# One tile per turn of TensorE's summing loop, its address in a register, instead of four tiles with constant addresses

## The chip, the core and the metric

The kernel runs on one core of one Trainium2 chip. The metric is the device time of the program in microseconds (us), taken from the slowest core, of which there is one. Kernels are compared only within the same rounds. A ratio is the mean time of one kernel's runs over the mean of the other's runs of the same rounds, so it is not quite the ratio of the medians that are quoted. The profile's span is about 1.8 us shorter than the time.

In the profile lines PE is TensorE, PEld its weight loads, DVE VectorE, ACT ScalarE, POOL GpSimd and SP SyncE. A q behind a name marks records of that engine's sequencer, the part that handles waits, register and branch instructions and the issue of DMAs; these do not count as busy time. L236 is line 236 of the kernel. `arena` is the on-chip buffer with the four slots.

## The reference

Every channel of a 384 x 384 x 384 picture in bfloat16 is scaled by a gate, which is a sigmoid of the channel's mean times one weight:

```python
def reference(x, w1d):                 # x: (1, 384, 384, 384), w1d: (1,)
    g = jnp.einsum("bhwc->bc", x) / (H * W)
    s = _sigmoid(g * w1d[0])           # k = 1, so the padding and the loop fall away
    return x * s[:, None, None, :]
```

The gate depends on all of x, so a plain program reads x twice. This one does not.

## The kernel before

It guesses. It takes the mean of the first 12 of 1152 rows (a row is 128 x 384 elements), computes the gate `s_early` from it, and gates and stores all of x with that, while TensorE sums all of x. At the end it computes the true gate `s_true`, rounded to bfloat16, and compares the two. Only where they differ does a second pass run; with these inputs they agree. So x is read once and written once: 226.5 MB in all.

The rows after the first 12 are 19 tiles of 60 rows. A tile is loaded by SyncE's DMA queue into one of four slots, summed by TensorE (45 matmuls of 128 x 512 against a matrix of ones, accumulated in three PSUM banks), gated in place by VectorE in two parts, and stored through ScalarE's queue. GpSimd tells TensorE with a semaphore `ready` that a tile has landed. VectorE may gate a part only when TensorE has summed it, and a slot is loaded again only when its store has landed. The last tile is gated into a free slot, so that it does not wait for TensorE.

The part of TensorE that the change touches:

```python
def add_rows(e, group, column, n, at_bank, start, stop):
    n_wide = n * C // WIDE                      # WIDE = 512
    for i in range(n_wide):
        out = mm(e, acc[group][(at_bank + i) % 3][:, :], ones[:],
                 arena[:, column + i * WIDE : column + (i + 1) * WIDE], ...)
    return out

def one(e, s):                                  # one tile; slot(s) is a constant
    e.wait_ge(ready, 1).then_inc(ready, -1)
    for r, n in parts:                          # 28 and 32 rows
        add_rows(e, 1, (slot(s) + r) * C, n, 0, False, False).then_inc(
            plan.sems["tensor"], 1)

with e.Fori(0, rounds) as k:                    # 5 rounds
    for s in range(some):                       # 3 tiles
        one(e, s)
    with e.If(k < rounds - 1):                  # a fourth in all but the last round
        for s in range(some, SLOTS):
            one(e, s)
```

At the end, ScalarE reads the flag of the comparison and then waits for the stores:

```python
second_pass("scalar", e)        # wait for the comparison, load the flag, branch
for token in plan.final:        # then one wait per store semaphore, two at a time
    e.wait_ge(*token)
```

## Time and profile before

| | before |
|---|---|
| time, median of 3 runs | 531.79 us (531.5 to 532.03) |
| span in the profile | 530.1 us |
| TensorE / VectorE busy | 43% / 46% |
| DMA, 13 to 509 us | share 1.00, 428 to 436 GB/s |
| last load landed, last sum begun | 509.0 us |
| flag computed | 526.8 us |
| last store landed | 529.6 us |

From the page of the kernel before: the span, the busy time of each engine, the busy tenths of the 16 DMA engines in 40 slices, and the DMA queues (queue, kind: packets, MB, share of 16 engines).

```profile
span 530.1 us, 1079 instructions
...
PE 227.4 (43%) x857; PEld 0.2 (0%) x2; DVE 241.5 (46%) x57; ACT 2.7 (1%) x4; POOL 0.3 (0%) x6
...
DMA  8999999999999999999999999999999999999996
...
q10 hardware_dynamic: 3314, 121.90, 53.2%
q1 hardware_dynamic: 2880, 104.60, 45.9%
q8 instruction: 1, 0.02, 0.0%
q14 instruction: 2, 0.02, 0.0%
```

The nines say that DMA is the limit from one end to the other. The q8 line, one packet of 0.02 MB, is an instruction fetch.

The table of stretches of the kernel before (from:to in us, its length, busy us with the number of instructions for PE, PEld, DVE, ACT and POOL, TensorE's granted clock as a share of full speed, DMA share, GB/s):

```profile
13.00:60.00 47.00, 26.84 (x103) 0.00 (x0) 24.25 (x11) 0.61 (x1) 0.00 (x0) 0.78 1.01 433
...
300.00:400.00 100.00, 47.62 (x177) 0.00 (x0) 45.62 (x8) 0.00 (x0) 0.00 (x0) 0.73 1.00 433
...
480.00:509.00 29.00, 0.00 (x0) 0.00 (x0) 10.83 (x3) 0.00 (x0) 0.00 (x0) 0.56 1.01 436
509.00:522.00 13.00, 12.92 (x48) 0.00 (x0) 6.52 (x1) 0.00 (x0) 0.00 (x0) 0.81 0.97 419
522.00:530.00 8.00, 0.03 (x1) 0.00 (x0) 3.79 (x9) 0.61 (x1) 0.00 (x0) 0.64 0.50 214
```

A DMA share of 1.00 beside a TensorE that is busy less than half of the time means that TensorE has slack in the middle. The end is another matter. The timeline of the kernel before from 505 us on (start, length, what; in brackets the idle time before it and what ended it), followed by ScalarE's ten waits for the stores:

```profile
508.96 6.56 DVE L199 TENSOR_TENSOR arena<-arena,s_early 128x12288 bf16<-128x12288 bf16 x1 [16.54 <-DMA arena<-in_x_dram]
509.08 12.30 PE L236 MATMUL acc<-arena,ones 128*128 128x512 bf16 x45 [31.13 <-PEq L275]
515.55 0.34 ACTq L109 DMA_DIRECT2D out_dram<-arena  x1
521.22 0.81 PE L236 MATMUL acc<-zeros,ones 128*128 128x512 bf16 x3
...
526.63 0.15 DVE L434 CAST redo<-wrong 128x1 int32<-128x1 f32 x1
```

```profile
L489 ACTq EVENT_SEMAPHORE  x10: 38/38/38, 527.8 to 529.6; - x10
```

Two chains run side by side from the moment that the last tile lands at 509.0. One is VectorE's gate (6.56 us) and the last store, issued at 515.55 and landed at 529.6. The other is TensorE's sum of the last tile, the closing matmuls, VectorE's and ScalarE's comparison, and the flag, done at 526.8; ScalarE then loads the flag and reaches its waits at 527.8. Nine of them are passed by 528.76; the last is passed at 529.65, when the store has landed. The page's own chain of waits names the flag's chain, since ScalarE's waits do not count as work; the time of the last wait shows which of the two was later.

### The profile page before, as it was taken

The numbers are of one execution on the slowest core, as the hardware profiler recorded it, in microseconds if no ns is written. First come the engines' busy times: TensorE is split into PE (matmuls) and PEld (weight loads), VectorE is DVE, ScalarE is ACT, GpSimd is POOL, SyncE is SP. The second block draws the span as 40 slices with busy tenths as digits, with TensorE's granted clock in tenths as the row PEclk, the third lists the DMA queues.
The fourth block names the chain that finished last, engine by engine and source line by source line (L and its number), as shares of the span: only waits on it lengthen the run. The fifth ranks groups of instructions, "written<-read, shape, count | busy, mean of one in ns | idle before, by whom it ended". The sixth has DMA issues, their size and how long they took to land. (4 is left out here: it accounts for less than half of the span.)

```text
span 530.1 us, 1079 instructions
## 1 busy us (share of the span) xinstructions
PE 227.4 (43%) x857; PEld 0.2 (0%) x2; DVE 241.5 (46%) x57; ACT 2.7 (1%) x4; POOL 0.3 (0%) x6
## 2 busy tenths in 40 slices
PE   2284971052434436262717080908080808070053
PEld 0000000000000000000000000000000000000000
DVE  0353997008080907172625353445344443538142
ACT  1000000000000000000000000000000000000000
POOL 0000000000000000000000000000000000000000
PEclk9786987568686958585858585859686868777567
DMA  8999999999999999999999999999999999999996
GB/s 361 445 445 404 408 445 438 421 431 435 445 428 428 431 435 445 431 424 435 435 445 431 424 428 442 445 428 428 428 442 445 424 431 424 445 420 458 418 421 299
DMA packets 6197, 226.53 MB, mean 427 GB/s; under 512 B 690, under 2 KB 690, under 8 KB 690
## 3 DMA queue, kind: packets, MB, share of 16 engines
q10 hardware_dynamic: 3314, 121.90, 53.2%
q1 hardware_dynamic: 2880, 104.60, 45.9%
q8 instruction: 1, 0.02, 0.0%
q14 instruction: 2, 0.02, 0.0%
HBM read 113.25 MB, written 113.25 MB: 427 GB/s over the span
## 5 line engine op out<-in xcount | busy, mean ns | idle before, releaser
L199 DVE TENSOR_TENSOR arena<-arena,s_early 128x10752 bf16<-128x10752 bf16 (+2 forms) x39 | 234.8, 6063 | 264.2 <-PE acc L236 245.3
L236 PE MATMUL acc<-arena,ones 128*128 128x512 bf16 x849 | 224.9, 429 | 285.0 <-PEq L275 283.6
L309 DVE TENSOR_TENSOR total<-total,acc 128x128 f32<-128x128 f32 (+2 forms) x11 | 4.5, 409 | 6.9 <-PE acc L236 6.5
L307 DVE COPY total<-acc 128x384 f32<-128x384 f32 x1 | 0.6, 558 | 11.4 <-PE acc L236 11.4
L234 PE MATMUL acc<-arena,ones 128*128 128x512 bf16 x1 | 0.6, 606 | 7.6 <-DMA arena<-in_x_dram 7.6
L412 ACT ACTIVATE s_true<-total,w_scaled 128x384 bf16<-128x384 f32 x1 | 0.6, 614 | 507.6 <-DVE total L309 507.6
L236 PE MATMUL acc<-zeros,ones 128*128 128x512 bf16 x6 | 2.3, 505 | 0.0
L338 ACT ACT_TABLE_LOAD x1 | 1.3, 1283 | 2.2 <-issue 2.2
L344 PE MATMUL w_all<-w_one,ones 1*128 1x1 bf16 x1 | 0.2, 158 | 2.0 <-DMA w_one<-in_w1d_dram 2.0
L420 DVE TENSOR_TENSOR total<-s_true,s_early 128x384 f32<-128x384 uint16 x1 | 0.6, 559 | 0.7 <-ACT s_true L412 0.7
L353 DVE TENSOR_SCALAR w_scaled<-w_all 128x1 f32<-128x1 f32 x2 | 0.2, 154 | 1.3 <-PE w_all L344 1.3
L375 ACT ACTIVATE s_early<-total,w_scaled 128x384 bf16<-128x384 f32 x1 | 0.6, 614 | 12.9 <-DVE total L309 12.9
L428 DVE TENSOR_REDUCE wrong<-total 128x1 f32<-128x384 f32 x1 | 0.6, 553 | 0.0
L362 DVE MEMSET ones<- 128x128 bf16 x1 | 0.2, 165 | 0.8 <-PEq L512 0.8
L338 ACT ACTIVATE warm<-warm 128x1 f32<-128x1 f32 x1 | 0.2, 203 | 0.0
L434 DVE CAST redo<-wrong 128x1 int32<-128x1 f32 x1 | 0.2, 153 | 0.0
L234 PEld LDWEIGHTS acc<-arena,ones 128*128 128x128 bf16 x1 | 0.1, 105 | 7.7 <-DMA arena<-in_x_dram 7.7
L344 PEld LDWEIGHTS w_all<-w_one,ones 1*128 1x128 bf16 x1 | 0.1, 101 | 2.0 <-issue 2.0
L512 POOL MEMSET const-bfloat16-1.0<- 128x1 bf16 x1 | 0.1, 101 | 0.0
L512 POOL MEMSET const-uint8-127<- 128x1 uint8 x1 | 0.1, 101 | 0.0
L361 POOL MEMSET zeros<- 128x2 bf16 x1 | 0.1, 99 | 0.0
L360 POOL MEMSET warm<- 128x1 f32 x1 | 0.1, 98 | 0.3 <-POOLq L512 0.3
(2 smaller groups left out, 0.2 us busy)
## 6 DMA issues: line engine op xcount, KB each, us to landing
out_dram<-arena ACTq DMA_DIRECT2D x18, 5760.0 KB, 53.5
arena<-in_x_dram SPq DMA_DIRECT2D x16, 5760.0 KB, 35.4
arena<-in_x_dram SPq DMA_DIRECT2D x2, 3072.0 KB, 37.3
arena<-in_x_dram ACTq DMA_DIRECT2D x1, 5760.0 KB, 45.1
out_dram<-arena ACTq DMA_DIRECT2D x1, 3072.0 KB, 14.1
arena<-in_x_dram ACTq DMA_DIRECT2D x1, 2688.0 KB, 18.7
arena<-in_x_dram SPq DMA_DIRECT2D x1, 2688.0 KB, 28.5
out_dram<-arena ACTq DMA_DIRECT2D x1, 2688.0 KB, 29.9
```

The lines of the kernel that those rows point to most:

```text
L199: return lambda e: e.tensor_tensor(to_v, v, s_b, ALU.mult)
L234: loaded.append(e.matmul(bank, weights, moving, start=start, stop=stop))
L236: return e.add_instruction(mybir.InstMatmult(name=nc.get_next_instruction_name(), engine=mybir.EngineType.PE, ins=[e.lower_ap(moving), e.l ...
L307: emit = lambda e, part=part, of=of: e.tensor_copy(part, of)
L309: emit = lambda e, part=part, of=of: e.tensor_tensor(part, part, of, ALU.add)
L338: lambda e: e.activation(warm[:, 1:2], warm[:, 0:1], ACT_F.Sigmoid),
L344: lambda e: e.matmul(w_all[:, 0:1], ones[0:1, :], w_one[0:1, 0:1], start=True, stop=True),
L353: lambda e, i=i, n=n: e.tensor_scalar_mul(w_scaled[:, i : i + 1], w_all[:, 0:1], 1.0 / float(P * n)),
L375: lambda e: e.activation(s_early[:], total[:], ACT_F.Sigmoid, scale=w_scaled[:, 0:1]),
L412: lambda e: e.activation(s_true[:], total[:], ACT_F.Sigmoid, scale=w_scaled[:, 1:2]),
L420: lambda e: e.tensor_tensor(total[:], s_true[:].bitcast(U16), s_early[:].bitcast(U16), ALU.not_equal),
L428: lambda e: e.reduce_max(wrong[:], total[:], axis=mybir.AxisListType.X),
```

## The change

Its intent is a short program: one tile in the loop body instead of four, with the tile's place in a register, so that TensorE's program is 115 instructions. The alignment of its start to a fetch block is dropped as no longer needed.

```diff
-    plan = Planner(nc, "a", 50)
+    plan = Planner(nc, "a", 60)
@@ add_rows
-                arena[:, column + i * WIDE : column + (i + 1) * WIDE],
+                arena[:, bass.ds(column + i * WIDE, WIDE)],
@@ sum_others
-            rounds = -(-n_tiles // SLOTS)
-            some = n_tiles - (rounds - 1) * SLOTS
-            with e.Fori(0, rounds) as k:
-                for s in range(some):
-                    one(e, s)
-                if some < SLOTS:
-                    with e.If(k < rounds - 1):
-                        for s in range(some, SLOTS):
-                            one(e, s)
+            with e.Fori(0, n_tiles) as k:
+                e.wait_ge(ready, 1).then_inc(ready, -1)
+                column = e.snap((k & (SLOTS - 1)) * (TILE * C))
+                for r, n in parts:
+                    add_rows(e, 1, column + r * C, n, 0, False, False).then_inc(
+                        plan.sems["tensor"], 1
+                    )
@@ tensor
-            e.addr_align(256, max_nops=0)
             plan.emit("tensor", e)
```

In the built program each of the 45 matmuls is preceded by one fused register instruction (add the offset, multiply by 2 to bytes, add the base) and takes its address from a register. All other engines keep their instructions and their order.

## The prediction

> **What bounds it now.** The DMA. In the table of stretches its share is 1.00 from 13 to 509 us; TensorE is busy 43% of the 530.1 us span. A tile's 45 matmuls take 10.5 to 13 us (timeline), tiles come 27 us apart. A store takes 53.5 us (median) from issue to landing while one is issued every 27 us, so about one whole store stands in the queue ahead of it: an estimated 25 us of slack before a later TensorE starves the DMA.
>
> Only the end depends on TensorE. The last tile lands at 509.0; its matmuls run from 509.08 to 521.2, three closing ones to 522.0, VectorE's and ScalarE's chain to 526.78; then ScalarE reads the flag (0.47 us), a fused register instruction (0.18), and from 527.75 to 529.65 its ten waits for the stores. Ten waits alone take about 0.8 us, so TensorE's chain has about 1.2 us of slack behind the last store.
>
> **What changes.** Five rounds of four (or three) tiles with constant addresses become 19 rounds of one. Bytes, matmuls, loads, gates, stores and the other engines' order stay. Added on TensorE's sequencer (the built program shows it): before each of the 45 matmuls a fused register instruction of three operations, and a matmul whose address is in a register; per tile one AND and one branch (0.08 to 0.21 us in the trace). The shorter program saves nothing visible: three instruction fetches in all, no stall at the branches.
>
> **Cost of issue.** Before, from the wait for a tile to the instruction after its 45 matmuls took 3.6 to 4.3 us: 80 to 95 ns per matmul, far ahead of the array (427 ns a matmul for the first dozen at clock 0.5, then 216). A fused instruction of three operations took 177 ns on ScalarE, 186 on SyncE; TensorE's sequencer leaves about 60 ns between instructions (two moves of 35 ns start 94 apart). Estimate: 180 + 60 + 90 = 330 ns a pair, more if a register address slows the matmul or this sequencer is slower (its semaphore events take 51 ns against 38): 370 taken, 300 to 450 possible. That exceeds 216, so TensorE becomes bound by its sequencer: 45 x 0.37 = about 16.7 us a tile. The wait blocks the sequencer, so nothing is done ahead.
>
> **On the critical path.** In the middle, +4 to 6 us per tile vanishes in idle time and the store queue's slack. At the end the last tile grows by about 4.8 us; minus 1.2 of slack, the end moves by 3.6 us. The Trainium skill ("TensorE: Matmul & The Clock Gate", "The two states you'll see") says that an idle array halves its clock; this trace agrees (0.5 at each tile's start). Gaps might keep it there; then 427 ns a matmul: 19.2 us, +6 us.
>
> **Predicted:** 535.4 us, 8 times in 10 between 532.0 and 539.5. Faster by over 2%: 0.01; within 2%: 0.93; slower by over 2%: 0.06.
>
> **What would show it.** Sequencer records of 177 to 260 ns between matmuls; tiles of 15 to 19 us in the timeline; DMA share still 1.00; in the chain that ended last, the last tile 15 to 19 us instead of 13. Wrong if tiles still take 11 to 12 us (then within 1 us of before), if a register matmul costs over 500 ns (over 2% slower), or if the loop straddles a fetch block and each branch waits for the busy DMA.

## The result and the profile after

The kernel after took 533.85 us (532.0 to 533.98, 4 runs) beside 531.91 us before (531.5 to 532.04, 4 runs): ratio 1.003, interval 1.0007 to 1.0052. That is within 2%, as forecast, and inside the range, but about half of the 3.6 us that the prediction derived. The profile shows that even this half did not come from where the prediction put it.

The same lines of the page of the kernel after:

```profile
span 532.1 us, 1984 instructions
...
PE 222.5 (42%) x852; PEld 0.2 (0%) x2; DVE 241.5 (45%) x57; ACT 2.7 (1%) x4; POOL 0.3 (0%) x6
...
DMA  9999999999999999999999999999999999999995
...
q10 hardware_dynamic: 3314, 121.90, 53.0%
q1 hardware_dynamic: 2880, 104.60, 45.8%
q14 instruction: 2, 0.02, 0.0%
```

The q8 fetch is gone. The table of stretches after, still with the DMA at 1.00 in the middle:

```profile
13.00:60.00 47.00, 24.85 (x95) 0.00 (x0) 21.13 (x5) 0.51 (x1) 0.00 (x0) 0.71 1.01 432
...
300.00:400.00 100.00, 44.94 (x176) 0.00 (x0) 45.07 (x8) 0.00 (x0) 0.00 (x0) 0.76 1.00 431
...
480.00:509.00 29.00, 0.53 (x2) 0.00 (x0) 12.25 (x3) 0.00 (x0) 0.00 (x0) 0.51 1.00 431
509.00:522.00 13.00, 11.34 (x47) 0.00 (x0) 7.11 (x5) 0.00 (x0) 0.00 (x0) 0.91 0.96 413
522.00:532.00 10.00, 0.00 (x0) 0.00 (x0) 2.31 (x6) 0.61 (x1) 0.00 (x0) 0.65 0.44 188
```

The timeline after from 505 us on, and ScalarE's ten waits:

```profile
508.09 6.56 DVE L199 TENSOR_TENSOR arena<-arena,s_early 128x12288 bf16<-128x12288 bf16 x1 [15.81 <-DMA arena<-in_x_dram]
508.47 11.27 PE L236 MATMUL acc<-arena,ones 128*128 x44 [29.98 <-PEq L278]
514.68 0.34 ACTq L109 DMA_DIRECT2D out_dram<-arena  x1
519.58 0.81 PE L236 MATMUL acc<-zeros,ones 128*128 128x512 bf16 x3
...
524.98 0.15 DVE L425 CAST redo<-wrong 128x1 int32<-128x1 f32 x1
```

```profile
L480 ACTq EVENT_SEMAPHORE  x10: 38/38/38, 526.6 to 531.6; - x10
```

The flag is ready at 525.1, which is 1.65 us *earlier* than before (its cast starts at 524.98 instead of 526.63), and TensorE's last tile took about 1 us less than before. ScalarE reaches its waits at 526.6 and then stands there until 531.6, for the last store. That store was issued at 514.68, before its counterpart in the kernel before (515.55), and landed 2 us later. So in these two executions the 2 us are lost in the DMA.

The 1.65 us add up. The last load landed 0.88 us earlier. The array ran about 7 matmuls at the half clock in place of 12, which saves an estimated 1.05 us (5 times 0.21); the issue was ahead of the array in both. From the wait to the first matmul it took 0.34 us in place of 0.08, with two register instructions in between that work out the first address: these 0.26 us are all that the change is seen to cost this chain. (The 44 matmuls in the line above are 45; one record is missing.)

The added instructions, on TensorE's sequencer in the kernel after (engine, operation, count: shortest, median and longest ns, first and last start in us):

```profile
L240 PEldq FUSED_REGOPS  x855: 46/46/46, 21.5 to 513.1; - x171
L240 PEldq ALU_OP  x19: 36/36/42, 21.3 to 508.3; - x19
```

The lines from which the prediction took its 180 ns, of the kernel before, and ScalarE's in the kernel after:

```profile
L464 SPq FUSED_REGOPS  x1: 186/186/186, 527.3 to 527.3; - x1
L464 ACTq FUSED_REGOPS  x1: 177/177/177, 527.3 to 527.3; - x1
```

```profile
L455 ACTq FUSED_REGOPS  x1: 179/179/179, 526.1 to 526.1; - x1
```

A fused instruction of TensorE took 46 ns, not 180. In the trace they start 104 ns apart with a matmul in between, so a pair costs 104 ns. For the last tile, 5.04 us pass from the wait to the instruction after the 45 matmuls; before, 4.32 us. The array needs 427 ns for each of its first matmuls and 216 ns later, so it is never short of work.

The DMA needed a view of its own. Each transfer lands in 16 parts, one per DMA engine. The landing times of the last store's 16 parts, from the trace's records:

```
            first    14th     15th     16th (last)    us from start
before     525.85   527.05   529.34   529.63
after      525.87   529.04   530.19   531.57
```

The median engine ends at 526.5 before and 526.3 after. The run waits for the slowest engines alone, and these were later. The median packet of 46080 bytes takes 1702 ns on an engine, and 226.5 MB at that rate fill 16 engines for an estimated 523 us. So there is little room to make good what delays one engine; the records do not name the engine of a packet, so this was not followed packet by packet. Packets more than 60 ns above the usual length for their size, between 70 and 505 us, sum up to 3.1 us over all engines before and to 10.4 us after, most of them single load packets.

### The profile page after: what moved, and what is told of

Same layout as the page of the kernel before. It is cut to its first block, busy times and chain, and to the rows that moved or that the text cites. A ratio compares the mean times of both kernels' runs of the same rounds, so it can differ in the third digit from the quotient of the medians.

```text
span 532.1 us, 1984 instructions
## 1 busy us (share of the span) xinstructions
PE 222.5 (42%) x852; PEld 0.2 (0%) x2; DVE 241.5 (45%) x57; ACT 2.7 (1%) x4; POOL 0.3 (0%) x6
## 5 line engine op out<-in xcount | busy, mean ns | idle before, releaser
L236 PE MATMUL acc<-arena,ones 128*128 (+1 forms) x844 | 220.7, 425 | 291.5 <-PEq L278 290.5
L234 PE MATMUL acc<-arena,ones 128*128 128x512 bf16 x1 | 0.6, 610 | 4.3 <-DMA arena<-in_x_dram 4.3
```

What stands on the lines that cost most here:

```text
L234: loaded.append(e.matmul(bank, weights, moving, start=start, stop=stop))
L236: return e.add_instruction(mybir.InstMatmult(name=nc.get_next_instruction_name(), engine=mybir.EngineType.PE, ins=[e.lower_ap(moving), e.l ...
```

## The experiments

Five questions: is a longer issue on TensorE absorbed, as predicted? Is the 2 us a property of the change or scatter? Does the fetch, the length of the instruction stream, or the phase between loads and stores explain it? The experiments ran in four jobs; each job has its own runs of the kernel before.

### Slow issue: the prediction's mechanism at a size that shows

Kernel after, with groups of three matmuls and an empty loop before most groups:

```diff
                 for r, n in parts:
-                    add_rows(e, 1, column + r * C, n, 0, False, False).then_inc(
-                        plan.sems["tensor"], 1
-                    )
+                    with e.Fori(0, n // 4 - 1) as g:
+                        with e.Fori(0, PAD):       # PAD = 2, later 1
+                            pass
+                        add_rows(e, 1, column + r * C + g * (4 * C), 4, 0, False, False)
+                    add_rows(
+                        e, 1, column + r * C + (n - 4) * C, 4, 0, False, False
+                    ).then_inc(plan.sems["tensor"], 1)
```

> The kernel after with its 45 register matmuls issued in groups of three, with an empty two-turn loop before most groups, so that a matmul costs the sequencer about 500 ns instead of the 104 measured after: tests the part of the prediction that the middle of the run absorbs a slow TensorE and only the last tile shows. If so: tiles of about 22 us in the middle with the DMA share still 1.00, last load still landing at 508 to 509, and the end late by the last tile's growth beyond the slack: about 508 + 22 + 9 = 539 us of span, 541 us of time. Rival (slower sums delay gates and stores all along): the last load lands many us later and the time is over 545 us.

Measured: 539.62 us (539.32 to 546.18), ratio 1.0194, 1.0138 to 1.0249, which is unclear at the 2% limit. From the wait to the instruction after its 45 matmuls the last tile took 21.64 us, 481 ns a matmul; the 553 ns that the next expectation names are those of its first groups of three. The middle of this kernel and its ten waits:

```profile
13.00:508.00 495.00, 245.59 (x810) 0.00 (x0) 230.73 (x40) 0.61 (x1) 0.00 (x0) 0.86 1.00 431
```

```profile
L485 ACTq EVENT_SEMAPHORE  x10: 38/38/38, 536.4 to 537.4; - x10
```

The last load still lands at 507.7 and the share is still 1.00, though TensorE needs some 22 us for a tile in place of 11 to 12. The ten waits now follow each other without a pause: the flag's chain ends the run, and every store has landed before, the last one at 532.0. ScalarE reached the waits at 536.4, 8.6 us later than in the kernel before. The middle was not entirely free: the median DMA engine ended at 529.1 instead of 526.3, since packets of all engines were held up around 80 us (perhaps because the first big stores then still wait for TensorE, which was not tested). That stays hidden behind the flag.

The next kernel has one empty turn instead of two:

> The slow-issue kernel with one empty turn instead of two per group: about 430 ns of sequencer per matmul, the upper part of the 300 to 450 that the prediction allowed. Theory (only the last tile shows, the prediction's mechanism with the wrong size): the flag chain ends about 40 x 0.12 = 4.8 us earlier than the 537.4 us measured at 553 ns, so about 533 us of span, the last store (529.5 to 532) no longer far behind it: 533 to 535.5 us of time. Rival (time rises in proportion to TensorE's busy time all along): in between, with the last load landing late.

Measured: 535.75 us (535.19 to 537.2) with before at 531.0 on this chip, ratio 1.0093, 1.0075 to 1.0111; 0.25 us above the range expected. The last tile's issue took 16.77 us, which is 373 ns a matmul, not 430, and is by accident nearly the 370 ns that the prediction assumed. Its ten waits, again without a pause:

```profile
L485 ACTq EVENT_SEMAPHORE  x10: 38/38/38, 531.9 to 532.9; - x10
```

At the issue cost that the prediction assumed, ScalarE reached its waits 4.2 us later than in the kernel before and passed the last one 3.3 us later; the prediction had 4.8 and 3.6. The times rose by 4.75 us. So the mechanism was right, and the size of one term was wrong. This kernel alone would not show it: in its trace the last store landed at 532.4, as late as in one trace of after (532.4), only 0.5 us before the last wait was passed. The kernel with two turns leaves 5.4 us between them.

### The alignment and the fetch

> The kernel after with the alignment put back, everything else as after. Theory A (the alignment costs an instruction fetch at the start, 2.05 us of one DMA engine in the trace of before and absent after; that sets which of the 16 engines lags, and so the last store): the fetch comes back, the first matmul starts near 9.8 us again instead of 6.5, and the time goes back to about 531.8 us. Theory B (twice as many sequencer instructions, recorded by the profiler, slow single DMA packets): stays at about 533.9. Theory C (two states that any kernel may fall in, whatever the change): a mixture of 532 and 534.

```diff
         def _(e):
+            e.addr_align(256, max_nops=0)
             plan.emit("tensor", e)
```

Measured: 531.87 us (530.84 to 536.85) with before at 531.31 (529.48 to 534.07, 11 runs on this chip), ratio 1.0024, 0.9986 to 1.0063: inconclusive for the time. The scatter of the kernel before on this chip, 4.6 us, was itself a finding: the half microsecond of the first job was luck. The start is clear, though. The queue line of this kernel, then the first matmul of before, after and this kernel from their timelines:

```profile
q8 instruction: 1, 0.02, 0.0%
```

```profile
9.79 0.61 PE L234 MATMUL acc<-arena,ones 128*128 128x512 bf16 x1 [7.58 <-DMA arena<-in_x_dram]
```

```profile
6.52 0.61 PE L234 MATMUL acc<-arena,ones 128*128 128x512 bf16 x1 [4.30 <-DMA arena<-in_x_dram]
```

```profile
9.06 0.61 PE L234 MATMUL acc<-arena,ones 128*128 128x512 bf16 x1 [6.87 <-DMA arena<-in_x_dram]
```

With the alignment the fetch is back and the first sum begins 2.5 us later than after. The packet is 16384 bytes, keeps one DMA engine for 1.4 to 2.05 us at about 2 us from the start, and so delays one of the 16 parts of the first load. No effect of it on the end of the run was seen.

> The kernel before without the alignment, else as before. Theory A: no fetch at 2.4 us, first matmul near 6.5 us, and the time goes up to about 533.9 us as after. Theory B: stays at 531.8. Theory C: a mixture of 532 and 534, with the kernel before mixed too.

```diff
         def _(e):
-            e.addr_align(256, max_nops=0)
             plan.emit("tensor", e)
```

Measured: 530.92 us (530.78 to 531.7), ratio 0.9994, 0.997 to 1.0019. The fetch moved to 70.4 us, the first matmul to 6.8, and the time did not rise, against theory A. Two runs follow of the kernel after with the alignment put back, in later jobs. Theories P, F and B of their expectations are explained at the run with the late refill, below.

> The kernel after with the alignment alone put back, again: the fetch at 2 us, the first refill near 79 us, phase 17.0, median near 531.9 by theory P and by F; 533.5 by rival B, as its instruction stream is as long as that of after.

> The kernel after with the alignment alone: phase of 17.0 us. Theory P: ratio 1.000 to 1.002. Rival: as after.

Measured: 531.66 us (530.27 to 533.69), ratio 1.0011, 0.999 to 1.0031, and 531.97 us (531.04 to 533.16), ratio 1.0003, 0.9979 to 1.0028. Both are below the kernel after of the same job and chip (532.15 and 532.39), but by less than the runs scatter. So it stays open whether what after may lose goes with the dropped alignment or with the loop and its register addresses.

### The length of the instruction stream

> The kernel before with an empty loop of 20 turns on TensorE's sequencer ahead of each tile's wait, in time where it idles: over 40 more recorded instructions per tile, about what the change adds, but aligned, with constant addresses and the fetch at the start. Theory B (recording slows single DMA packets): about 533.9 us, with isolated slow packets through the run. Theory A: 531.8 us. Theory C: a mixture.

```diff
         def one(e, s):
+            with e.Fori(0, 20):
+                pass
             e.wait_ge(ready, 1).then_inc(ready, -1)
```

Measured: 531.72 us (530.8 to 535.37), ratio 1.0013, 0.9979 to 1.0047. The median is that of before; two of six runs are above 534 us, and the profiled one, among them, has 6.3 us of slow packets. Together with the aligned kernel (as many instructions as after, and 0.5 to 2.2 us of slow packets in its three traces) this speaks against theory B, but does not exclude a small part of it.

### Is it the change at all?

> The kernel after, unchanged, again. Theory C (the 2 us by which after was slower is the scatter of the slowest DMA engine, not the change): ratio to before within 0.4% of 1, runs of both kernels scattered over 529.5 to 534, and the span in the trace equal to the median engine's last landing (526.3) plus the slowest engine's lag plus 0.4 us. Rival (the change costs 2 us): about 533.5 us with before at 531.3, ratio 1.003 to 1.005.

Measured: 533.93 us (530.4 to 537.9), before 531.0, ratio 1.0045, 1.0008 to 1.0081.

> The kernel after with 50 DMA semaphores in the pool as before instead of 60: under 50 DMAs are issued, so no semaphore is reused in either and nothing should move. Theory C: as the unchanged kernel after, within 0.4% of before. Rival (a change of semaphore numbers matters): differs from the unchanged kernel after by over 1 us.

```diff
-    plan = Planner(nc, "a", 60)
+    plan = Planner(nc, "a", 50)
```

Measured: 532.9 us (532.02 to 538.84), ratio 1.0053, 1.0017 to 1.0089; its median is 1.03 us below that of the kernel after on the same chip, by the letter just over the limit of 1 us set for the rival, but with six runs each that scatter over some 7 us, and their means agree within 0.1 us. The number of semaphores does nothing that these runs can show. By its own rule theory C fails here: both ratios are above 1.004, and the kernel after scatters over 7.5 us while before keeps to 1.8 us.

### The phase between loads and stores

The traces suggested a cause. In each run, stores land a constant time behind the loads, when each landing is taken at the median of its 16 parts; this time is called the phase here. The kernel after, which did not fetch, had a phase of 20.4 us; those that fetched, at 2 or at 70 us, had 13.7 or 17.0. Theory P says that the phase is set when SyncE issues the first refill, which waits for the slowest part of the first big store (in the kernel before it landed at 80.87 us, and the refill was issued at 80.89). In these two kernels SyncE pauses once at that point:

```diff
+            if k == SLOTS:
+                for token in plan._needs([], rows(slot(k), TILE)):
+                    plan._wait("sync", token)
+                plan.streams["sync"].append(("block", pause, None))
             if k < last:
                 load(slot(k), TILE, row0(k))
     # pause: with e.Fori(0, TURNS): pass       TURNS = 6 or 14
```

> The kernel after, with SyncE pausing for an empty loop of 6 turns (1 to 2 us) once, between the landing of the first big store and the first refill load that it releases; nothing else changed, no fetch at the start. Theory P (phase): in the traces so far the first refill is issued at 80.9 us (before), 78.9 to 79.2 (the three aligned or unaligned variants that fetched) or 77.8 (after), which leaves the stores landing 13.7, 17.0 or 20.4 us behind the loads for the rest of the run; in the phase of 20.4 single load packets are slow (8 to 10 us summed over all engines from 70 to 505 us, against 1.6 to 6.3) and the slowest engine ends later. So a later refill must give a phase of 17.0, fewer slow packets, and a median near 531.5 instead of 533.5. Rival B (the longer instruction stream): phase may move, but the time stays near 533.5. Rival F (the absence of the fetch itself): the same.

> The same with 14 turns (about 3 us): by theory P a phase of 13.7 us as in the kernel before, and a median near 531 to 532. Rivals: 533.5.

> The kernel after unchanged on the same chip as the other three: phase 20.4 us, median 532.5 to 534, with runs up to 538.

Measured on one chip, with before at 531.51 us: six turns 531.98 us, ratio 1.0019 (1.0001 to 1.0036); 14 turns 531.97 us, ratio 1.0011 (0.9996 to 1.0026); the unchanged kernel after 532.15 us (532.05 to 532.69), ratio 1.0017 (1.0001 to 1.0032). The control did not show the 532.5 to 534 us expected of it, so there was little for the pause to gain. The last call, on the same chip, asked the question once more:

> The kernel after once more: phase of 20.4 us, five or more us of isolated slow packets; ratio to before 1.002 to 1.005. Theory P says that it is the slowest of the three kernels of this call; rival (the phase moves packets about but not the end) says that the three agree within 0.1%.

> The kernel after with the pause of 14 turns again: phase of 13.6 us, about 2 us of isolated slow packets. Theory P: ratio to before at least 0.2% below that of after (0.999 to 1.002). Rival: the same as after.

Measured, with before at 531.86 us: after 532.39 us, ratio 1.002 (0.9989 to 1.005); 14 turns 532.21 us, ratio 1.0009 (0.9984 to 1.0033). The ratios are in theory P's order, but after is 0.11% above the paused kernel in place of 0.2%, and the intervals overlap.

What the traces of these runs say of the DMA, worked out from their packet and landing records (us; the phase is the median over the middle of the run of a store's landing less the landing of the load before it, each at its median part; "slow" is the sum of the excess defined above):

| kernel | fetch at | first refill issued | phase | slow | median / slowest engine's last landing |
|---|---|---|---|---|---|
| before | 2.4 | 80.9 | 13.7 | 3.1 | 526.5 / 529.6 |
| before, unaligned | 70.4 | 79.0 | 17.0 | 2.3 | 526.3 / 528.6 |
| before, longer stream | 1.9 | 79.2 | 17.0 | 6.3 | 526.3 / 531.9 |
| after | none | 77.8 | 20.4 | 10.4 | 526.3 / 531.6 |
| after, again | none | 77.8 | 20.4 | 8.4 | 526.4 / 532.4 |
| after, 50 semaphores | none | 77.9 | 20.4 | 9.7 | 526.4 / 530.4 |
| after, control | none | 77.7 | 20.3 | 5.2 | 526.2 / 530.1 |
| after, third | none | 77.8 | 20.3 | 5.7 | 526.3 / 529.8 |
| after, 6 turns | none | 79.4 | 17.0 | 2.0 | 526.3 / 529.6 |
| after, 14 turns | none | 81.3 | 13.6 | 1.6 | 526.3 / 529.8 |
| after, 14 turns, again | none | 81.6 | 13.6 | 10.4 | 527.1 / 530.6 |
| after, aligned (three runs) | 1.9 to 2.2 | 78.8 to 78.9 | 17.0 to 17.2 | 0.5 to 2.2 | 526.3 to 526.4 / 528.6 to 529.6 |
| slow issue, one turn | none | 78.0 | 20.3 | 10.3 | 526.3 / 532.4 |
| slow issue, two turns | none | 77.8 | 20.4 | 35.5 | 529.1 / 532.0 |

The first half of theory P is shown: the instant of the first refill sets the phase for the whole run, and a pause of 1.5 or 3.5 us moved it from 20.4 to 17.0 or 13.6 us, with no other change. The three values lie 3.4 us apart, twice the 1.70 us of a packet. The second half, that the phase sets the slow packets and the end, fell. The phase of 13.6 occurred once with 1.6 us of slow packets and once with 10.4, and the times of the kernels on one chip overlap. In the second of these traces (span 532.6 us) the slow engine also brought the last load only at 511.9, so that the flag's chain ended the run there. Slow packets and the end of the run thus vary from run to run in the same kernel and the same phase.

What stays open: after was slower than before in all four comparisons (1.003, 1.0045, 1.0017, 1.002), though the last interval includes 1. Taken over all jobs, 21 runs of after have a median of 532.7 us and 48 of before one of 531.5, so some 0.2 to 0.3% may be real. In the four traces of after the last store ends the run, so it lies at the slowest DMA engine, not in TensorE's chain. What makes a single packet slow there, no run here could tell.

## Why the prediction was right or wrong

- **What bounds the kernel: right.** DMA share 1.00 in the middle before and after, and the last load landed at 508.1 after against 509.0 before.
- **"TensorE becomes bound by its sequencer": wrong, and this is the step that failed.** The term was 180 + 60 + 90 = 330 ns a pair, taken as 370. Measured were 104 ns a pair, under half of the array's 216. The 180 ns were read off ScalarE's and SyncE's fused instruction, which compares and combines; TensorE's, which adds and multiplies, took 46 ns. In the same trace of after, ScalarE's still took 179 ns. Whether the engine or the operations make the difference, no run separates. Moreover the 90 ns a matmul were added whole: before, 80 to 95 ns covered the whole step from one matmul to the next, and after, the fused instruction and its matmul together took only 104. The prediction had named this outcome: wrong if tiles still take 11 to 12 us.
- **"The last tile grows by about 4.8 us": did not happen.** It took 11.3 us for its matmuls instead of 12.3. The array ran about its first 7 matmuls at the half clock after (427 ns each, then 216) and its first 12 before. The Trainium skill ("TensorE: Matmul & The Clock Gate", section "The two states you'll see") says that the window which decides on the clock runs freely, so that the point of change depends on where in it the first matmul falls. The traces agree: in both, all changes of the granted clock lie on one grid of 3.41 us, and the change came 4.9 us after the tile's first matmul before and 2.9 us after it in the kernel after. So the gain of 1 us is taken here as luck; the address form gives no reason for it.
- **What is absorbed in the middle, and that only the end shows: right,** and shown by a slower issue: at 373 ns a matmul the time is 535.75 us, at 481 ns 539.62 us, with the last load on time in both (508.1 and 507.7) and ScalarE at its waits 4.2 and 8.6 us later. The estimate of 25 us of slack was rough: at 481 ns the median DMA engine ended 2.8 us later, after packets held up near 80 us.
- **"TensorE's chain has about 1.2 us of slack behind the last store": nearly right for before,** where ScalarE paused 0.9 us before the last wait. It missed that the other side of that sum, the last store, is no constant: the slowest DMA engine ended 2.2 to 6.1 us after the median one.
- **"The shorter program saves nothing visible": nearly right.** Short and without the alignment, it saves a fetch and brings the first sum 3.3 us forward, and no time at the end. The dropped alignment takes part in this: aligned, the same short program fetched at about 2 us.
- **The time:** inside the range and within 2%, for another reason than the one given. Of the 1.9 us of the first comparison none came through TensorE in the profiled executions.

## What to carry to other kernels

Cost an added instruction by the same operation on the same engine, or call the estimate what it is, a guess with a wide factor; and ask first what the consumer's rate is: here an issue of 104 ns a matmul, below the array's 216, cost only the 0.26 us before the first matmul of a tile. Where DMA is saturated and a store ends the run, as in all traces of after, the run ends with the slowest of the 16 engines, so look at the parts of the last landing before looking for the lost microseconds in the engine that was changed. Three runs within 0.1% on one chip are no measure of the scatter: the same kernel spread over 0.9% on the next.

## What the Trainium skill lacked or had wrong

- "Advanced Engine Details and Errata" (section "Control Flow Timing") gives about 108 ns for compare-and-branch. On TensorE's sequencer it took 67 to 77 ns when not taken and about 208 to 228 ns when taken; on SyncE's it took 40 to 45 ns, and an empty turn cost 0.25 us there.
- No page gives the cost of a matmul whose address is in a register. Here the fused register instruction took 46 ns and the pair with its matmul 104 ns on TensorE; a fused instruction of five operations took 125 ns (in the slow-issue kernels), and one with comparisons 177 to 203 ns on ScalarE, SyncE and VectorE.
- "DMA: Bandwidth & Descriptors" (section "Latency and other measured facts") has two of the 16 DMA engines as usually slower and, as a best guess, puts that down to software-generated descriptors. The data queues here are of the kind hardware_dynamic, and in every trace the slowest engine still ended 2.2 to 6.1 us after the median one. The records do not name the engine, so whether it is one of those two stays open.
- "Runtime: NRT & Kernel Launch" (section "Instruction fetch mechanics") calls crossing a 16 KiB block mostly hidden. The trace agrees with the size (one packet of 16384 bytes) and, for the end of the run, with "hidden"; but beside the first loads the packet held one engine for up to 2.05 us and delayed the first matmul from 6.5 to 9.1 us (after, without and with the alignment).
- No page tells that the instant of one refill can fix the phase of loads and stores for a whole run (13.6, 17.0 or 20.4 us here).
